# Fused attention, dense layer and routed experts: one attention chunk started a block later, expert weight splits at fixed places in the last dense group, and 13 expert steps of 256 with 2 of 128 in place of 12 with 4

## The chip, the cores and the metric

The kernel runs on one core of one Trainium2 chip. The metric is the device time of one execution in microseconds (us). TensorE (PE) does the matmuls and transposes, ScalarE (ACT) the activations and copies, VectorE (DVE) the elementwise work, GpSimd (POOL) the indirect transfers of rows, and SyncE (SP) issues the other transfers.

## What is computed

```python
f = sigmoid(f_logit)                        # q, k, v, f: 4 x 8 x 768 x 48
state = f[t] * state + outer(k[t], v[t])    # for each batch and head, t = 0..767
y[t] = q[t] @ state
x = y as rows                               # 3072 tokens of 384
h = maximum(x @ w_in, 0); x = (h * h) @ w_out          # 384 -> 2048 -> 384
logits = x @ w_gate; e = argmax(logits); gate = softmax(logits)[e]
out[token] = gate * (maximum(x @ w1[e], 0) @ w2[e])    # 8 experts, 384 -> 1024 -> 384
```

A token goes through one expert only. With the inputs of the reference the eight experts get 648, 242, 82, 602, 407, 692, 240 and 159 tokens; the kernel doesn't know this beforehand and computes its lists on the chip.

## The kernel before

**Attention** is done in 24 chunks of 128 tokens, three to a group of 384. `scores(c)` transposes the scaled keys (`pk`) and multiplies scaled queries with them (`pa`), `masked(c)` applies the causal mask on VectorE, `outputs(c)` makes the rows `y`, `state(c)` carries the state on, `decays(c)` and `scale_qk(c)` prepare the decay products of a chunk and scale its queries and keys by them. Chunks 0 to 2 are done before the main loop.

**The dense layer** follows in eight groups `g` of 384 tokens, each in 16 blocks `i` of 128 hidden columns: `moe_h` makes `ph`, `moe_act` on ScalarE `gg` (relu, square) and its parts `gh` and `gl`, `moe_out` two blocks later adds to three accumulators `po`. In group 0 the products run in plain fp32 on `w_raw`; meanwhile the weights, which come as 64-bit words, are staged (`stage_job`), made into `w_raw` on VectorE (`convert_job`, three instructions each, 16 jobs, the last 13 one in each block) and, eight blocks later, split into a rounded part `w_hi` (ScalarE copies) and the rest `w_lo` (VectorE subtracts). From group 1 on each product is the sum of three: high by high, high by low, low by high.

While the blocks of group `g` run, `attention_group(g + 1)` makes the input of the next group: a chunk starts in block `b` (`scores`, `masked`), goes on with `decays` of the next in `b + 1`, with `outputs` and `state` in `b + 2` and `scale_qk` of the next in `b + 3`. Here `b` is 0, 5 and 10 for the three chunks. `route(g)` makes the routing of the group before: small products `pl` with the gate weights, the choice of an expert, counts (`pc`) and a table of slots (`pslot`).

**The experts** run in steps of one expert each, listed in `KINDS`: a step `D` takes 256 rows and splits both weight matrices as above, a step `S` takes 128 rows and runs its first product in plain fp32 from the raw weights `rawt`, its second one split. Each has eight blocks (`step_h`: `ph`, `hh`, `hl`; `step_out`: `qo` or `qs`). A step's weights are eight parts `j` of 384 KB; `load_w` fetches a part into `rawt[j]`, `split_part` splits it into `w_hi` and `w_lo`, and only then the same buffer can be loaded for the next step. The first two steps (`NEARLY`) use counts of the groups before the last, so that their parts are loaded and split while the last dense group still runs. `lookup` and the other tables give the rows of all later steps (`pi`). Rows come and go by indirect transfers.

Of the steps in `KINDS` the last three ran only if the counts needed them (`rest`, in `extra_steps`); 12 `D` and 4 `S` always ran. A pair of halves that finds no `D` takes two `S`.

**Order.** Up to the end of the last dense group the order on PE, ACT, DVE and POOL is that of the code. In the first two steps PE's order was that of the code and the other engines' was chosen by the scheduler; from step 2 on PE and ACT keep the order of the code. In the steps the splits are placed by `split_plan`, which goes through the blocks with an assumed time for each and places a split when its load, with 4 us assumed, is due.

Of the kernel before, what the change touches and what calls it, by code (L numbers as in the profile page):

```python
# [19 lines left out]
B, H, S, D = 4, 8, 768, 48  # L20
# [12 lines left out]
ROW = DM + 1  # L33
CAP = NT
SB = 256
KINDS = "DD" + "DDDSDDSDDSDDDS" + "SSS"
NSTEP = len(KINDS)
NBLK = NE * CAP // SB
NALWAYS = NSTEP - 3
ND = KINDS.count("D") - 2  # L40
NS = KINDS.count("S")
NEARLY = 2
# [14 lines left out]
def gla_moe_moe_kernel(ctx: ExitStack, tc: tile.TileContext, qk, ft, vt, w_in, w_out, w_gate, w_gateT, w_e, q, k, v, f_logit, out, dbg=None):  # L57
# [129 lines left out]
    def convert_job(n):  # L187
        if n < len(jobs):
            w_raw[jobs[n]] = t = wlp.tile([128, WP], F32, tag="w", name="w_raw")
            narrow(t.bitcast(U32), staged.pop(n).bitcast(U32).rearrange("p (b two) -> p b two", two=2))  # L190
            stage_job(n + 3)
# [168 lines left out]
    def attention_group(g):  # L360
        for m in range(GC):
            c = g * GC + m
            b = 5 * m
            while not (yield) == (b, 1):
                pass
            if m == 0:
                x_tiles(g)
            if 4 < c + 2 < NCH:
                load_chunk(c + 2)
            scores(c)  # L370
            masked(c)
            sigmoid(c + 1)
            while not (yield) == (b + 1, 0):
                pass
            if c + 1 < NCH:
                decays(c + 1)
            while not (yield) == (b + 2, 1):
                pass
            state(c, outputs(c))
            while not (yield) == (b + 3, 0):  # L380
                pass
            if c + 1 < NCH:
                scale_qk(c + 1)
        while not (yield) == (14, 0):
            pass
        split_x(g)
        yield
# [210 lines left out]
    convert_job(1)  # L598
    decays(3)
    state(2, pu)  # L600
    convert_job(2)
    scale_qk(3)
    job = 3

    ph2 = ExitStack()
# [95 lines left out]
    def open_right():  # L701
# [42 lines left out]
        load_x(0)  # L744
        load_x(1)

    pend = []
    rt_gen = None

# [15 lines left out]

    for g in range(NG):
        att = Piece(attention_group(g + 1)) if g + 1 < NG else None
        if g == NG - 1:
            right = open_right()
        for i in range(NF):  # L770
            ph = moe_h(g, i)
            if att:
                att.at(i, 0)
            if rt_gen and 2 <= i <= 10 and g < NG - 1:
                next(rt_gen, None)
            if g == 0 and job < len(jobs):
                convert_job(job)
                job += 1
                if job == len(jobs):
                    phs.close()  # L780
                    wgp = pha.enter_context(tc.tile_pool(name="wgp", bufs=1, side="right", reuse_waits="tile"))
                    wgb = [wgp.tile([128, NE, DM], F32, name="wgb")]
                    early["ab"] = [wgp.tile([128, NBLK + SB], F32R, name=f"ab{m}") for m in range(GC)]
                    nc.sync.dma_start(out=wgb[0], in_=w_gateT[None, :, :].to_broadcast([128, NE, DM]))
            pend.append((g, i, *moe_act(g, ph)))
            n = g * NF + i - 8
            split_job(n)
            if n == len(jobs) - 1:
                wst_.extend([[w_hi[w][:, j], w_lo[w, j]] for j in range(NP)] for w in range(2))
            if len(pend) > 2:  # L790
                done = flush_one()
                if done is not None:
                    rt_gen = route(done)
                    next(rt_gen)
            if att:
                att.at(i, 1)
            if g == NG - 1:
                if i < 2:
                    next(right, None)

                for j in {5: [0], 7: [1], 9: [2], 10: [3], 11: [4], 13: [5], 15: [6, 7]}.get(i, ()):
                    split_part(*wst_[0][j], rawt[j])
                    load_w(1, j)
                if i == 13:
                    prep_step(0, *early["x0"])
            if rt_gen and i >= 2 and (i > 10 or g == NG - 1):
                next(rt_gen, None)
        if rt_gen:
            for _ in rt_gen:
                pass  # L810
            rt_gen = None
# [130 lines left out]
        nc.vector.tensor_tensor(out=need, in0=need, in1=over[:, 1:2], op=ALU.add)  # L942
        nc.vector.scalar_tensor_tensor(out=tot, in0=need, scalar=0.0, in1=bad, op0=ALU.max, op1=ALU.add)

    early["split"], early["ready"] = [], False
    SPLITS = split_plan()

    def split_w(s, j):
# [119 lines left out]
        if s < NEARLY:  # L1068
            next(fin, None)

    with tc.manual_schedule(engines={mybir.EngineType.PE}):
        left = run_steps(0, NEARLY, hook, flush=False)
    with tc.manual_schedule(engines={mybir.EngineType.PE, mybir.EngineType.Activation}):
        run_steps(NEARLY, NALWAYS, pend=left)
    more = nc.values_load(tot[0:1, 0:1], min_val=0, max_val=NSTEP + GENERAL)
    ph2.close()
    both.close()
    with tc.If(more > NS - 3, label="rest"):
        extra_steps(tc, ident, xs, x_esi, x_ids, w_e, out)
        with tc.If(more > GENERAL - 1):  # L1080
            general_path(tc, ident, rev, narrow, q, k, v, f_logit, w_in, w_out, w_gate, w_e, out)
# [4 lines left out]
def split_plan():  # L1086
# [3 lines left out]
            slots.append((clock, s, i))  # L1090
            clock += 2.0 if kind == "D" else 1.2
    begin = {(s, i): t for t, s, i in slots}
    ready, plan = {(1, j): 0.0 for j in range(8)}, {}

    def release(s, j, t):
        if s < NALWAYS:
            ready[s, j] = max(t + 4.0, begin[1, 2] if s == NEARLY else 0.0)

    for t, s, i in slots:
        if KINDS[s] == "S" and i % 2:  # L1100
            release(s + 1, i // 2, t)
# [265 lines left out]
```

## Time and profile before

| | |
|---|---|
| median of 3 runs | 817.12 us (816.12 to 817.61) |
| profiled execution | 815.93 us, of which the span on the core is 814.2 |
| TensorE busy | 782.8 us, 96% of the span |
| VectorE, ScalarE busy | 558.1 and 413.9 us |

The page lists what one profiled execution did. The busy share of an engine includes time at a reduced clock; for TensorE a window gives the granted clock as a fraction of full speed. A row of a timeline has its start, its duration, its engine and line, the tiles, and in brackets the idle time of the engine before it with what ended that.

### The profile page before, as it was taken

What the parts mean: (1) busy time and instruction counts of PE and PEld (TensorE: products, weight loads), DVE (VectorE), ACT (ScalarE), POOL (GpSimd) and SP (SyncE); (2) the same over time, 40 slices, a digit from 0 to 9 for tenths busy, and PEclk for the clock granted to TensorE, in tenths of its full rate; (3) what the DMA queues carried; (4) which work ended last, traced back from release to release, by engine and by line L of the source; (5) the groups of instructions that cost most, each with busy time, mean ns of one, the idle gap of its engine ahead of it and who ended that gap; (6) DMA issues with size and microseconds to landing.
All of it is one profiled execution on the core that took longest, in us unless ns stands there. A gap on an engine that the chain in (4) does not pass through costs nothing.

```text
span 814.2 us, 15228 instructions
## 1 busy us (share of the span) xinstructions
PE 782.8 (96%) x5681; PEld 728.7 (89%) x5681; DVE 558.1 (69%) x1315; ACT 413.9 (51%) x830; POOL 78.1 (10%) x109
## 2 busy tenths in 40 slices
PE   5699999999999999999999999999999999999995
PEld 4556569999999999999999999999999999999995
DVE  7988859767757757857757844668567565757651
ACT  2223466454454455455455454662566566556651
POOL 2000000000000000000000002000423312313111
PEclk9899999999999999999999999999999999999998
DMA  9975330121130121131120015321867686868730
GB/s 262 245 245 180 130 70 25 46 80 45 44 101 25 45 81 46 44 85 41 45 70 1 1 39 195 106 78 45 326 208 215 216 281 195 292 204 291 226 112 30
DMA packets 40564, 102.10 MB, mean 125 GB/s; under 512 B 5630, under 2 KB 9442, under 8 KB 40352
## 3 DMA queue, kind: packets, MB, share of 16 engines
q1 hardware_dynamic: 36896, 91.57, 37.2%
q0 software_dynamic: 3584, 9.46, 3.1%
q8 instruction: 47, 0.77, 0.4%
q14 instruction: 37, 0.30, 0.1%
HBM read 91.31 MB, written 10.24 MB: 125 GB/s over the span
## 4 chain that ended last, share of the span: by engine, by line
PE 75%; issue 8%; DMA 7%; DVE 4%; ACT 3%; POOL 1%; SPq 0%; POOLq 0%; DVEq 0%; ACTq 0%
PE po L434 22%; PE ph L404 21%; PE qo L997 9%; PE ph L977 8%; DMA raw<-w_e 5%; PE ph L394 4%; PE pa L263 3%; PE py L319 3%; ACT w_hi L612 2%; PE py L299 1%; PE pu L309 1%; DVE w_lo L613 1%; DMA out<-o,ids 1%; DMA xT<-xT 1%; PE pk L256 1%
## 5 line engine op out<-in xcount | busy, mean ns | idle before, releaser
L410 ACT ACTIVATE gg<-ph 128x384 f32<-128x384 f32 x128 | 62.8, 491 | 181.0 <-PE ph L404 128.1
L613 DVE TENSOR_TENSOR w_lo<-raw,w_hi 128x768 fp32r<-128x768 f32 x112 | 106.9, 956 | 47.8 <-ACT w_hi L612 44.0
L404 PE MATMUL ph<-xh,w_lo 128*128 128x384 f32 x336 | 118.6, 353 | 1.4 <-ACT gg L410 1.4
L417 DVE TENSOR_TENSOR gl<-gg,gh 128x384 fp32r<-128x384 f32 x112 | 62.0, 554 | 78.4 <-ACT gh L415 74.4
L404 PE MATMUL ph<-xl,w_hi 128*128 128x384 f32 x336 | 114.4, 340 | 0.6 <-DVE xl L162 0.6
L434 PE MATMUL po<-w_hi,gl 128*128 128x384 f32 x336 | 113.5, 338 | 1.5 <-DVE gl L417 1.5
L404 PE MATMUL ph<-xh,w_hi 128*128 128x384 f32 x336 | 113.8, 339 | 0.0
L434 PE MATMUL po<-w_hi,gh 128*128 128x384 f32 x336 | 113.2, 337 | 0.0
L434 PE MATMUL po<-w_lo,gh 128*128 128x384 f32 x336 | 112.7, 336 | 0.0
L612 ACT ACTIVATE w_hi<-raw 128x768 fp32r<-128x768 f32 x112 | 93.8, 839 | 21.2 <-DMA raw<-w_e 20.6
L981 ACT ACTIVATE hh<-ph 128x256 fp32r<-128x256 f32 (+1 forms) x128 | 45.4, 356 | 91.2 <-PE ph L977 67.4
L977 PE MATMUL ph<-xh,w_lo 128*128 128x256 f32 x288 | 82.6, 287 | 0.6 <-DVE w_lo L613 0.6
L458 DVE SCALAR_TENSOR_TENSOR junk<-rows,wgb 128x384 f32<-128x384 f32 x144 | 79.8, 554 | 3.3
L977 PE MATMUL ph<-xl,w_hi 128*128 128x256 f32 x288 | 81.2, 282 | 0.0
L977 PE MATMUL ph<-xh,w_hi 128*128 128x256 f32 x288 | 81.0, 281 | 0.0
L982 DVE SCALAR_TENSOR_TENSOR hl<-ph,hh 128x256 fp32r<-128x256 f32 (+1 forms) x128 | 49.4, 388 | 45.2 <-ACT hh L981 40.9
L404 PEld LDWEIGHTS ph<-xh,w_lo 128*128 128x128 f32 x336 | 63.0, 187 | 7.4 <-issue 3.1
L411 ACT ACTIVATE gg<-gg 128x384 f32<-128x384 f32 x128 | 67.2, 525 | 4.0
L997 PE MATMUL qo<-w_hi,hl 128*128 128x384 f32 x192 | 66.1, 344 | 1.0 <-ACT o L1009 1.0
L997 PE MATMUL qo<-w_hi,hh 128*128 128x384 f32 x192 | 65.1, 339 | 0.0
L997 PE MATMUL qo<-w_lo,hh 128*128 128x384 f32 x192 | 65.0, 338 | 0.0
L434 PEld LDWEIGHTS po<-w_hi,gl 128*128 128x128 f32 x336 | 63.0, 188 | 2.1 <-DVE gl L417 1.8
(235 smaller groups left out, 1534.4 us busy)
## 6 DMA issues: line engine op xcount, KB each, us to landing
raw<-w_e SPq DMA_DIRECT2D x128, 384.0 KB
qk<-qk SPq DMA_DIRECT2D x46, 192.0 KB
v<-vt SPq DMA_DIRECT2D x24, 256.0 KB
stg<-w_in SPq DMA_DIRECT2D x8, 768.0 KB
stg<-w_out SPq DMA_DIRECT2D x8, 768.0 KB
f<-ft SPq DMA_DIRECT2D x24, 226.2 KB
xs<-rows SPq DMA_DIRECT2D x8, 577.5 KB
wgb<-w_gateT SPq DMA_DIRECT2D x1, 1536.0 KB
```

The costliest lines, as they stand in the source:

```text
L404: nc.tensor.matmul(ph, lhsT=w[:, sl], rhs=x[:, k, :], start=(n == 0), stop=(n == 8))
L410: nc.scalar.activation(out=gg, in_=ph, func=AF.Relu)
L411: nc.scalar.activation(out=gg, in_=gg, func=AF.Square)
L417: nc.vector.tensor_tensor(out=gl, in0=gg, in1=gh.bitcast(F32), op=ALU.subtract)
L434: nc.tensor.matmul(po[m], lhsT=a[:, sl], rhs=w[:, ws], start=(i == 0 and n == 0), stop=(i == NF - 1 and n == len(terms) - 1),)
L458: nc.vector.scalar_tensor_tensor(out=junk, in0=rows[:, m, 0:DM], scalar=1.0, in1=wgb[0][:, e, :], op0=ALU.mult, op1=ALU.mult, accum_out=lg ...
L612: nc.scalar.activation(out=hi, in_=src, func=AF.Copy)
L613: eng.tensor_tensor(out=lo, in0=src, in1=hi.bitcast(F32), op=ALU.subtract)
L977: nc.tensor.matmul(ph, lhsT=wslice(s, w, (i * 3 + k) * 128, 128), rhs=x[:, k, :], start=(n == 0), stop=(n == 8))
L981: nc.scalar.activation(out=hh, in_=ph, func=AF.Relu)
L982: nc.vector.scalar_tensor_tensor(out=hl, in0=ph, scalar=0.0, in1=hh.bitcast(F32), op0=ALU.max, op1=ALU.subtract)
L997: nc.tensor.matmul(out_t[s][m], lhsT=x[:, sl], rhs=wslice(s, w, 3 * F2 + i * DM, DM), start=(i == 0 and n == 0), stop=(i == 7 and n == 2),)
```

## The change

It has three parts. First, the chunks of group 1's attention start in blocks 1, 6 and 10 of group 0 (0, 5 and 10 before), and the scaling of chunk 3 is written ahead of conversion 2. Second, the list of steps always run has 13 `D` and 2 `S`, with the two `S` at its end, and four instead of three more steps wait behind the condition. Third, a table `AHEAD` says which part of which of the first two steps is split in which block of the last dense group: (0, 3) is part 3 of step 0. Six parts of step 1 are now in it, and ACT's order in the first two steps is that of the code. `split_plan` places only parts 6 and 7 of step 1, and lets splits for step 2 begin at block 4 of step 1, not 2.

```diff
--- before.py
+++ after.py
@@ -33,10 +33,11 @@
 ROW = DM + 1
 CAP = NT
 SB = 256
-KINDS = "DD" + "DDDSDDSDDSDDDS" + "SSS"
+NEXTRA = 4
+KINDS = "DD" + "DDDDDDDDDDDSS" + "S" * NEXTRA
 NSTEP = len(KINDS)
 NBLK = NE * CAP // SB
-NALWAYS = NSTEP - 3
+NALWAYS = NSTEP - NEXTRA
 ND = KINDS.count("D") - 2
 NS = KINDS.count("S")
 NEARLY = 2
@@ -360,7 +361,7 @@
     def attention_group(g):
         for m in range(GC):
             c = g * GC + m
-            b = 5 * m
+            b = (1, 6, 10)[m] if g == 1 else 5 * m
             while not (yield) == (b, 1):
                 pass
             if m == 0:
@@ -598,8 +599,8 @@
     convert_job(1)
     decays(3)
     state(2, pu)
+    scale_qk(3)
     convert_job(2)
-    scale_qk(3)
     job = 3
 
     ph2 = ExitStack()
@@ -744,6 +745,8 @@
         load_x(0)
         load_x(1)
 
+    AHEAD = {4: [(0, 0)], 5: [(0, 1)], 6: [(0, 2)], 7: [(1, 0)], 8: [(0, 3), (1, 1)], 9: [(1, 2)], 10: [(0, 4)]}
+    AHEAD |= {11: [(1, 3)], 12: [(0, 5)], 13: [(1, 4)], 14: [(0, 6)], 15: [(0, 7), (1, 5)]}
     pend = []
     rt_gen = None
 
@@ -798,9 +801,11 @@
                 if i < 2:
                     next(right, None)
 
-                for j in {5: [0], 7: [1], 9: [2], 10: [3], 11: [4], 13: [5], 15: [6, 7]}.get(i, ()):
-                    split_part(*wst_[0][j], rawt[j])
-                    load_w(1, j)
+
+                for t, j in AHEAD.get(i, ()):
+                    split_part(*wst_[t][j], rawt[j])
+                    if t == 0:
+                        load_w(1, j)
                 if i == 13:
                     prep_step(0, *early["x0"])
             if rt_gen and i >= 2 and (i > 10 or g == NG - 1):
@@ -942,7 +947,7 @@
         nc.vector.tensor_tensor(out=need, in0=need, in1=over[:, 1:2], op=ALU.add)
         nc.vector.scalar_tensor_tensor(out=tot, in0=need, scalar=0.0, in1=bad, op0=ALU.max, op1=ALU.add)
 
-    early["split"], early["ready"] = [], False
+    early["split"], early["ready"] = [j for js in AHEAD.values() for t, j in js if t == 1], False
     SPLITS = split_plan()
 
     def split_w(s, j):
@@ -1068,14 +1073,14 @@
         if s < NEARLY:
             next(fin, None)
 
-    with tc.manual_schedule(engines={mybir.EngineType.PE}):
+    with tc.manual_schedule(engines={mybir.EngineType.PE, mybir.EngineType.Activation}):
         left = run_steps(0, NEARLY, hook, flush=False)
     with tc.manual_schedule(engines={mybir.EngineType.PE, mybir.EngineType.Activation}):
         run_steps(NEARLY, NALWAYS, pend=left)
     more = nc.values_load(tot[0:1, 0:1], min_val=0, max_val=NSTEP + GENERAL)
     ph2.close()
     both.close()
-    with tc.If(more > NS - 3, label="rest"):
+    with tc.If(more > NS - NEXTRA, label="rest"):
         extra_steps(tc, ident, xs, x_esi, x_ids, w_e, out)
         with tc.If(more > GENERAL - 1):
             general_path(tc, ident, rev, narrow, q, k, v, f_logit, w_in, w_out, w_gate, w_e, out)
@@ -1090,12 +1095,14 @@
             slots.append((clock, s, i))
             clock += 2.0 if kind == "D" else 1.2
     begin = {(s, i): t for t, s, i in slots}
-    ready, plan = {(1, j): 0.0 for j in range(8)}, {}
+    ready, plan = {(1, j): 0.0 for j in (6, 7)}, {}
 
     def release(s, j, t):
         if s < NALWAYS:
-            ready[s, j] = max(t + 4.0, begin[1, 2] if s == NEARLY else 0.0)
-
+            ready[s, j] = max(t + 4.0, begin[1, 4] if s == NEARLY else 0.0)
+
+    for j in range(6):
+        release(NEARLY, j, 0.0)
     for t, s, i in slots:
         if KINDS[s] == "S" and i % 2:
             release(s + 1, i // 2, t)
```

On VectorE, just before the main loop and in its first block, before. L166, L169 and L172 are one conversion, L234 to L236 the scaling of chunk 3, L270 its masking:

```order
43 L166 TENSOR_SCALAR w_raw<-stg 128x768
44 L169 SCALAR_TENSOR_TENSOR w_raw<-stg,w_raw 128x768
45 L172 SCALAR_TENSOR_TENSOR w_raw<-stg,w_raw 128x768
46 L234 TENSOR_TENSOR qk_148<-qk_148,tl 112x512
47 L235 TENSOR_TENSOR qk_148<-qk_148,f 112x512
48 L236 TENSOR_TENSOR pmin<-pmin,tl 112x4
49 L166 TENSOR_SCALAR w_raw<-stg 128x768
50 L169 SCALAR_TENSOR_TENSOR w_raw<-stg,w_raw 128x768
51 L172 SCALAR_TENSOR_TENSOR w_raw<-stg,w_raw 128x768
52 L270 TENSOR_TENSOR at<-pa,mask 128x512 x2
```

The same place of the changed kernel; its lines have a number one higher:

```order
43 L235 TENSOR_TENSOR qk_148<-qk_148,tl 112x512
44 L236 TENSOR_TENSOR qk_148<-qk_148,f 112x512
45 L237 TENSOR_TENSOR pmin<-pmin,tl 112x4
46 L167 TENSOR_SCALAR w_raw<-stg 128x768
47 L170 SCALAR_TENSOR_TENSOR w_raw<-stg,w_raw 128x768
48 L173 SCALAR_TENSOR_TENSOR w_raw<-stg,w_raw 128x768
49 L167 TENSOR_SCALAR w_raw<-stg 128x768
```

The scaling has moved ahead of conversion 2. The masking, ahead of which two conversions stood, follows as row 55, behind three.

On TensorE at the same place before: L394 is `ph` in group 0, L256 and L263 are the scores of chunk 3, L434 is `po`, L299 the first part of its outputs:

```order
53 L394 MATMUL ph<-xT_186,w_raw 128x384 x3
54 L256 MATMUL pk<-ident,qk_148 128x112 x4
55 L263 MATMUL pa<-qk_148 128x128 x8
56 L394 MATMUL ph<-xT_186,w_raw 128x384 x6
57 L434 MATMUL po_489<-w_raw,gg 128x384
58 L434 MATMUL po_490<-w_raw,gg 128x384
59 L434 MATMUL po_491<-w_raw,gg 128x384
60 L299 MATMUL py<-qk_148,wst_106 64x128 x8
```

After:

```order
53 L395 MATMUL ph<-xT_186,w_raw 128x384 x6
54 L257 MATMUL pk<-ident,qk_148 128x112 x4
55 L264 MATMUL pa<-qk_148 128x128 x8
56 L395 MATMUL ph<-xT_186,w_raw 128x384 x3
57 L435 MATMUL po_489<-w_raw,gg 128x384
58 L435 MATMUL po_490<-w_raw,gg 128x384
59 L435 MATMUL po_491<-w_raw,gg 128x384
60 L395 MATMUL ph<-xT_186,w_raw 128x384 x3
61 L435 MATMUL po_489<-w_raw,gg 128x384
62 L435 MATMUL po_490<-w_raw,gg 128x384
63 L435 MATMUL po_491<-w_raw,gg 128x384
64 L300 MATMUL py<-qk_148,wst_106 64x128 x8
```

Two blocks of `ph` now run ahead of the scores, and two blocks of `po` with a `ph` between them ahead of the outputs.

On ScalarE in the last blocks of group 7 and the first of step 0, before. L410, L411 and L415 are the activation of a dense block, L612 is a `w_hi` copy (154 and 155 are the buffers of the two steps' weights, the numbers of `raw` its parts), L451 takes the last accumulators, L981 is `hh` of a step and L476 the copy `xt` in the routing:

```order
538 L415 ACTIVATE gh<-gg 128x384
539 L612 ACTIVATE w_hi_155<-raw_5246 128x768
540 L410 ACTIVATE gg<-ph 128x384
541 L411 ACTIVATE gg<-gg 128x384
542 L415 ACTIVATE gh<-gg 128x384
543 L612 ACTIVATE w_hi_154<-raw_5247 128x768
544 L612 ACTIVATE w_hi_154<-raw_5248 128x768
545 L451 ACTIVATE rows<-po_5385 128x384
546 L451 ACTIVATE rows<-po_5387 128x384
547 L612 ACTIVATE w_hi_155<-raw_5247 128x768
548 L981 ACTIVATE hh<-ph_5912 128x256
549 L476 ACTIVATE xt_5258<-pt 128x384
```

After (its L613 is the same copy, L986 is `hh`):

```order
538 L416 ACTIVATE gh<-gg 128x384
539 L613 ACTIVATE w_hi_154<-raw_5247 128x768
540 L411 ACTIVATE gg<-ph 128x384
541 L412 ACTIVATE gg<-gg 128x384
542 L416 ACTIVATE gh<-gg 128x384
543 L613 ACTIVATE w_hi_154<-raw_5248 128x768
544 L613 ACTIVATE w_hi_155<-raw_5246 128x768
545 L452 ACTIVATE rows<-po_5385 128x384
546 L452 ACTIVATE rows<-po_5387 128x384
547 L986 ACTIVATE hh<-ph_5924 128x256
548 L613 ACTIVATE w_hi_155<-raw_5247 128x768
549 L477 ACTIVATE xt_5258<-pt 128x384
```

The copy of part 6 of step 0 now comes a block earlier (row 539), and a copy for step 1 no longer directly precedes the activation of the next block with its raw part just requested.

On VectorE in the first blocks of step 0, before. L513 to L518 belong to the routing of group 7, L654 and L656 to the tables of the later steps, L982 is `hl` of a step's block:

```order
713 L513 TENSOR_REDUCE sf<-sl 128x3
714 L654 TENSOR_TENSOR gt_6098<-cnt,jj_6096 128x96
715 L654 TENSOR_TENSOR gt_6104<-cnt,jj_6102 128x96
716 L515 CAST si<-sf 128x3
717 L931 TENSOR_REDUCE ctot<-cnt 128x1
718 L656 TENSOR_REDUCE nb_6100<-gt_6098 128x8
719 L656 TENSOR_REDUCE nb_6106<-gt_6104 128x8
720 L517 TENSOR_SCALAR hl<-si 128x3
721 L518 TENSOR_SCALAR hl<-si 128x3
722 L982 SCALAR_TENSOR_TENSOR hl<-ph_6034,hh 128x256
```

After:

```order
707 L514 TENSOR_REDUCE sf<-sl 128x3
708 L987 SCALAR_TENSOR_TENSOR hl<-ph_6044,hh 128x256
709 L655 TENSOR_TENSOR gt_6104<-cnt,jj_6102 128x96
710 L655 TENSOR_TENSOR gt_6110<-cnt,jj_6108 128x96
711 L516 CAST si<-sf 128x3
712 L936 TENSOR_REDUCE ctot<-cnt 128x1
713 L657 TENSOR_REDUCE nb_6106<-gt_6104 128x8
714 L657 TENSOR_REDUCE nb_6112<-gt_6110 128x8
715 L518 TENSOR_SCALAR hl<-si 128x3
716 L519 TENSOR_SCALAR hl<-si 128x3
```

`hl` of block 3 (`hl<-ph_6034` before, `hl<-ph_6044` after) has moved from behind the routing's shifts to a place ahead of `gt`.

## Rows read from the trace of the kernel before

**Rows 1.** Page, part 1: busy time of each engine, share of the span, instructions.

```profile
PE 782.8 (96%) x5681; PEld 728.7 (89%) x5681; DVE 558.1 (69%) x1315; ACT 413.9 (51%) x830; POOL 78.1 (10%) x109
```

**Rows 2.** Waits of TensorE: us in total, times, longest.

```profile
PE pk L256 <- issue: 4.8, 1, 4.8
PE po L434 <- DVE gl L417: 1.5, 1, 1.5
...
PE qo L997 <- ACT o L1009: 1.0, 1, 1.0
```

**Rows 3.** Timeline of TensorE, 28 to 62 us.

```profile
30.00 2.20 PE L394 MATMUL ph<-xT,w_raw 128*128 128x384 f32 x6 [0.64 <-ACT xT L332]
37.02 0.98 PE L256 MATMUL pk<-ident,qk 112*128 112x112 f32 x4 [4.82 <-issue]
...
39.94 5.87 PE L394 MATMUL ph<-xT,w_raw 128*128 128x384 f32 x12
...
47.67 0.67 PE L299 MATMUL py<-qk,wst 48*64 48x128 f32 x16
...
49.75 2.20 PE L394 MATMUL ph<-xT,w_raw 128*128 128x384 f32 x6
...
53.73 2.10 PE L394 MATMUL ph<-xT,w_raw 128*128 128x384 f32 x6
```

**Rows 4.** Timeline of VectorE, 32 to 40 us.

```profile
33.78 0.55 DVE L166 TENSOR_SCALAR w_raw<-stg 128x768 uint32<-128x768 uint32 x1
...
36.23 0.68 DVE L234 TENSOR_TENSOR qk<-qk,tl 112x512 f32<-112x512 f32 x1
...
37.51 0.55 DVE L166 TENSOR_SCALAR w_raw<-stg 128x768 uint32<-128x768 uint32 x1
```

**Rows 5.** Windows: length, busy by engine (PE, PEld, DVE, ACT, POOL), PEclk, DMA, GB/s.

```profile
36.60:43.50 6.90, 6.48 (x26) 4.49 (x27) 6.80 (x12) 1.07 (x2) 0.00 (x0) 0.51 0.71 233
...
106.00:110.00 4.00, 2.07 (x7) 0.94 (x6) 1.36 (x1) 2.81 (x5) 0.00 (x0) 1.00 0.12 26
```

**Rows 6.** Waits of VectorE from 32 to 96 us.

```profile
DVE at L270 <- PE pa L263: 5.0, 2, 4.7
DVE w_lo L162 <- ACT w_hi L161: 1.2, 3, 0.4
```

**Rows 7.** Timeline of TensorE: the preparations of steps 2, 4, 11 and 15.

```profile
582.69 0.82 PE L641 MATMUL px<-ident,xg 128*128 128x128 f32 x6
...
617.81 0.82 PE L641 MATMUL px<-ident,xg 128*128 128x128 f32 x6
...
726.48 0.49 PE L1034 MATMUL px<-ident,xg 128*128 128x128 f32 x3
...
789.03 0.49 PE L1034 MATMUL px<-ident,xg 128*128 128x128 f32 x3
```

**Rows 8.** Chain that ended last, 520 to 552 us: start, us, what.

```profile
545.32 3.27 DMA raw<-w_e
```

**Rows 9.** Timeline of ScalarE, 538 to 556 us.

```profile
541.23 0.85 ACT L612 ACTIVATE w_hi<-raw 128x768 fp32r<-128x768 f32 x1 [2.05 <-DMA raw<-w_e]
...
548.61 0.84 ACT L612 ACTIVATE w_hi<-raw 128x768 fp32r<-128x768 f32 x1 [2.02 <-DMA raw<-w_e]
```

**Rows 10.** Timeline of TensorE: `pl` of group 6, and of group 7.

```profile
499.67 2.07 PE L484 MATMUL pl<-wg,xt 128*128 128x8 f32 x18
...
549.03 0.73 PE L484 MATMUL pl<-wg,xt 128*128 128x8 f32 x6
...
551.99 0.52 PE L977 MATMUL ph<-xh,w_lo 128*128 128x256 f32 x1
```

**Rows 11.** Window 552 to 556 us, columns as in rows 5.

```profile
552.00:556.00 4.00, 4.00 (x27) 3.84 (x26) 2.38 (x13) 0.61 (x2) 0.00 (x0) 0.57 0.01 4
```

**Rows 12.** Timeline of VectorE, 553 to 575 us.

```profile
556.87 0.43 DVE L654 TENSOR_TENSOR gt<-cnt,jj 128x96 f32<-128x96 f32 x2
...
557.80 0.42 DVE L982 SCALAR_TENSOR_TENSOR hl<-ph,hh 128x256 fp32r<-128x256 f32 x1
```

## Prediction

> **What bounds the kernel now.** I read the busy times of the page first: TensorE is busy 782.8 us of 814.2, 96% [rows 1], so the time is the length of TensorE's own work plus its few waits and the stretches in which its clock is granted at half. The second view is therefore the list of TensorE's waits. Apart from the start, where nothing is changed, four of them lie where the change works: 4.8 us before the transposes `pk`, 1.5 us before `po`, 1.0 us before `qo` and (in the third part below) short ones before `pl` [rows 2]. The third view is the timeline around each, the fourth the windows that give the granted clock. Three places remain, and I cost them apart: attention chunk 3 in dense group 0, the list of expert steps, and the passage from the last dense group into the first expert steps.
>
> **Part 1: chunk 3 a block later, its scaling before conversion 2.** TensorE finishes block 0's `ph` near 32.2, waits 4.82 us for the transposes of chunk 3 and only then goes on [rows 3]. What is late is VectorE: it does conversion 2 (33.78 to 36.23) before it scales `kd` (from 36.23, 0.68) [rows 4]. "issue" as the releaser only says that the profile shows no nearer event; the end of the `kd` row at 36.9 fits the start at 37.02. During the wait and just after it the granted clock falls to half, 1.2 GHz: 0.51 over 36.6 to 43.5 [rows 5]. Work of 6.9 us at 0.51 would take 3.4 us less at full clock.
>
> I rebuild the stretch row by row in the new order. One block of `ph` and `po` takes 53.73 − 49.75 = 3.98 us at full clock, so a `ph` about 2.0 [rows 3]. Blocks 0 and 1 of `ph` now come first and end near 34.0. On VectorE the scaling takes the place of conversion 2: `kd` is ready at 33.78 + 0.68 = 34.5. A wait of 0.5 us is left. Scores took 39.94 − 37.02 = 2.92 us at half clock, so about 1.5 at full: until 36.0. Block 2's `ph` needs conversion 2, which now follows the three scaling rows: 33.78 + 1.28 + 2.45 = 37.51 [rows 4], a second wait of 1.5 us. Then `ph`, `po`, `ph`, `po` (7.96), the outputs of chunk 3 (49.75 − 47.67 = 2.08 [rows 3]) and `ph` of block 4 starts at 37.51 + 10.04 = 47.55, where it started at 53.73 before. **Gain 6.2 us.**
>
> The moved step takes its loads along: chunk 5's load is issued one block later on SP's queue, and its data are first read with chunk 4's scores, five blocks behind. Conversion 2 ends 1.3 us later, so does the issue of staging load 5; conversion 5 now comes after two more conversions, the masking and the scans of chunk 4, so that load keeps over 6 us. The masking of chunk 3 now stands behind conversions 3 and 4 (2.45 each): 37.51 + 4.9 = 42.4, done by 43.7; its reader, the outputs of chunk 3, is due at 45.5.  Is the gain given back later, because VectorE can't follow? From 32 to 96 us, up to the last conversion, its two largest waits are 5.0 us for `pa` and 1.2 for `w_hi` [rows 6]. So VectorE could end that conversion at most some 6.2 us earlier, which just covers the gain: after that it has no idle time left. The loads of the gate weights and of `xT` follow the last conversion and move with it.
>
> **Part 2: two steps of 128 become one of 256.** A step of 256 takes (617.81 − 582.69)/2 = 17.56 us between preparations of its rows. From 726.48 to 789.03 there are three of them and one of 128: 62.55 − 52.68 = 9.87 [rows 7]. Two of these less one of 256 is **2.18**. From 617.81 to 726.48 there are five of 256 and two of 128: 108.67 − 87.80 = 20.87, which is 1.13 over 2·9.87. A step of 128 may so cost the steps behind it something. After the change the steps of 128 are the last two, with no step of 256 behind them, so I take it that **1.13** goes too (0 at the least). Together 3.3 us. At nothing I cost: the wider step's splits and x rows (the ten such steps of before run at 17.56 with them); the weight load, one step fewer; the two adjoining steps of 128, where a load is issued per odd block and is wanted about a step later, and a load took 3.27 us [rows 8]. If that cover were gone, one load, 3.3 us, would show.
>
> Weighed against the Trainium skill ("FP8 and Floating Point Precision", TensorE Precision Notes): true fp32 goes through the array four times. Counted in columns at 2.4 GHz this gives 8·(2·(3·512 + 3·384) − (9·256 + 6·384)) = 6144 columns, an estimate of 2.56 us where the rows give 2.18; by it the gain of this part would be 3.7.
>
> **Part 3: the splits for steps 0 and 1 at fixed places.** In the last blocks of group 7 ScalarE waits 2.05 us at 541.23 in front of a `w_hi` copy whose raw weights are still on their way [rows 9]; the load behind it takes 3.27 us from release to landing [rows 8]. Everything queued behind it on ScalarE is late, first the activation of block 15, so TensorE waits 1.50 us before `po` [rows 2]. At 548.61 it happens again, 2.02 us [rows 9]; now the copy of `xt` is late, and the 18 small `pl` matmuls take 551.99 − 549.03 = 2.96 us where the group before needed 2.07 [rows 10]: 0.9. Right after, the window 552 to 556 has a granted clock of 0.57 [rows 11]; 0.86 of it at half is 3.4 us, 1.7 us lost. Later ScalarE takes a copy for step 2 ahead of `o`, and `qo` waits 0.96 [rows 2]. In the new order a block or more of other work always stands between a load and its copy, two or three in the last group, where a block takes over 3 us of TensorE time: the loads land in that time. Copies for step 2 start two blocks later, behind both `o`. So 1.5 + 0.9 + 1.7 + 1.0 = 5.1 may go.
>
> What comes in: VectorE's new order has `hl` of block 3 ahead of the two `gt` of the step tables. Before, `gt` began at 556.87 and this `hl` at 557.80 [rows 12]. VectorE must now stand until then, 0.9 us; everything on the chain to `pslot` is that much later. The bounds are 0 (TensorE reaches `pslot` early enough behind) and 0.9; the chain was tight, I take 0.75. The same lateness meets `pi`, which TensorE already waited for a little: again 0 to 0.9, I take 0.75. **Net 5.1 − 1.5 = 3.6 us,** bounds 1.5 (the clock stays low and both are paid in full) and 5.1. SP's scalar reads for the expert numbers are now ahead of step 3's loads only, and the writing of the last rows comes later; both have a step of slack.
>
> **Sum.** 6.2 + 3.3 + 3.6 = 13.1. The profiled execution took 815.93, so 802.8. The median of the three runs, 817.12, is 1.2 above it; on it the forecast is 804.0. A change under 0.2%, 1.6 us, could hardly be told from none here.
>
> **Rivals.**
>
> *The clock falls all the same.* In part 1 0.5 + 1.5 us of waiting remain within 3.6 us. For it: at 552 the clock fell after far less waiting. Against it: from 106 to 110 TensorE is busy only 2.07 of 4.00 us and keeps a clock of 1.00 [rows 5], nearly the same share. If it falls, up to 3.4 us are lost in part 1 (807.4); if it stays low in part 3, 1.7 (805.7). The Trainium skill ("TensorE: Matmul & The Clock Gate", What's actually happening) says that the slow clock is the default and activity releases it. By that rule a wait that is merely shortened can still cost the clock; 106 to 110 is a row where it did not, 552 one where it did.
>
> *VectorE or the staging loads bound group 0.* For it: VectorE's two gaps are all it can give [rows 6]. Against it: conversions run ahead of their readers, which is why `pa` let VectorE wait 5.0 us. If a staging load is late by one conversion (2.45), or the end of conversion 15 moves by half of those 6.2 only, part 1 gives 3 to 3.8, some 3.5: 806.7.
>
> *The new waits eat part 3.* If the chain to `pslot` and `pi` is late by more than the one `hl` (each further `hl` ahead of it waits for a block of TensorE, about 2 us), part 3 gives 0.5: 807.1.
>
> *The conditional rest runs: slower.* The always-run list holds 13 steps of 256 and 2 of 128. The routed counts of the reference's inputs are 648, 242, 82, 602, 407, 692, 240, 159: two pairs in early steps, 11 more and 2 single halves. Before, 10 pairs fitted and the eleventh took two steps of 128, four of four; now 11 of 11 and 2 of 2. It decides at a third half: then four extra steps of 128 run after all others. At 9.87 us each, their loads hidden, they add 39.5: 802.8 + 39.5 + 1.2 = 843.5, and more if the loads show. Both lists are filled exactly, so only an error in my count brings this.
>
> **How the numbers follow.** Forecast as summed 0.58; clock falls in part 1 or 3 0.15; VectorE or loads in group 0 0.10; new waits 0.12; rest runs or something of that size 0.03; the remaining 0.02 for no difference that can be told, for which every part would have to fail. The likeliest case alone spans 801.5 (part 3 at 5.1, part 2 at 3.7) to 806. The range 801 to 808 takes in the three rivals of the same sign with their single prices and leaves out two of them together. Faster 0.95, same 0.02, slower 0.03.
>
> **What would show it.** Part 1: `ph` of block 4 starts near 47.5, two waits of 0.5 and 1.5 stand in place of 4.82, and the clock is 1.00 from 32 to 48. Part 2: 17.56 between preparations throughout, 9.9 per step of 128 at the end. Part 3: no ScalarE wait on `raw` behind 538, `po` and `qo` out of the list of waits, `pslot` and `pi` in it with 0.7 to 1.3 each. I'm wrong if the clock is at half after chunk 3, if conversions trail their loads, or if a chain of table rows holds TensorE for over 2 us in step 0 or 1.

## The result

The changed kernel takes 804.95 us in the median of 4 runs (803.46 to 805.68), the kernel before 816.91 in the runs beside it; the ratio is 0.9864, 95% interval 0.9846 to 0.9881. Forecast were 804.0, within 801 to 808. The profiled execution took 804.5 us, with a span of 802.8 where it was 814.2: 11.4 us less, where 13.1 were forecast.

Four places of TensorE's timeline cut the span into stages: the first product of group 1, the preparations of steps 0 and 2, and the last matmul. In the changed kernel:

```profile
102.46 0.45 PE L405 MATMUL ph<-xh,w_lo 128*128 128x384 f32 x1 [0.88 <-ACT gg L411]
...
527.71 0.82 PE L642 MATMUL px<-ident,xg 128*128 128x128 f32 x6
...
572.07 0.82 PE L642 MATMUL px<-ident,xg 128*128 128x128 f32 x6
...
765.23 0.49 PE L1039 MATMUL px<-ident,xg 128*128 128x128 f32 x3
...
791.13 0.34 PE L1002 MATMUL qs<-w_hi,hh 128*128 128x384 f32 x1
```

The same rows of the kernel before that were not shown yet:

```profile
108.75 0.44 PE L404 MATMUL ph<-xh,w_lo 128*128 128x384 f32 x1 [1.36 <-ACT gg L410]
...
534.00 0.82 PE L641 MATMUL px<-ident,xg 128*128 128x128 f32 x6
...
805.05 0.34 PE L997 MATMUL qs<-w_hi,hh 128*128 128x384 f32 x1
```

| stage | before | after | less by | forecast |
|---|---|---|---|---|
| start to first product of group 1 | 108.75 | 102.46 | 6.29 | 6.2 |
| to the preparation of step 0 | 425.25 | 425.25 | 0.00 | 0 |
| to that of step 2 | 48.69 | 44.36 | 4.33 | 3.6 |
| to the end of the last matmul | 222.70 | 219.40 | 3.30 | 3.3 |
| to the end of the span | 8.81 | 11.33 | −2.52 | 0 |

TensorE was to end 13.1 us earlier and ended 13.9 earlier. Behind it 2.5 us were lost, in a stage that the prediction costed at nothing.

Timeline of TensorE at chunk 3, after; the rows answer to [rows 3]:

```profile
30.07 4.14 PE L395 MATMUL ph<-xT,w_raw 128*128 128x384 f32 x12 [0.64 <-ACT xT L333]
34.64 0.58 PE L257 MATMUL pk<-ident,qk 112*128 112x112 f32 x4 [0.43 <-PE ph L395]
35.29 1.16 PE L264 MATMUL pa<-qk 48*128 48x128 f32 x16
37.82 2.17 PE L395 MATMUL ph<-xT,w_raw 128*128 128x384 f32 x6 [1.37 <-DVE w_raw L173]
...
47.81 2.20 PE L395 MATMUL ph<-xT,w_raw 128*128 128x384 f32 x6
```

Two waits of 0.43 and 1.37 stand in place of 4.82 (forecast 0.5 and 1.5), and block 4 starts at 47.81 (forecast 47.55, before 53.73). That is 5.92 us earlier; the stage gains 6.29 mainly because the wait before the first product of group 1 also shrank, from 1.36 to 0.88. The first row covers two blocks of `ph`, which now run without a break. The window over the stretch that had a clock of 0.51 [rows 5]:

```profile
36.60:43.50 6.90, 5.68 (x18) 3.46 (x19) 6.73 (x10) 1.02 (x2) 0.00 (x0) 1.00 0.69 217
```

At the passage into the expert steps, the list of TensorE's waits has one row, and the small routing products are one group again, as long as in the group before; they answer to [rows 2] and [rows 10]:

```profile
PE pi L673 <- DVE sel L669: 1.2, 1, 1.2
```

```profile
540.94 2.07 PE L485 MATMUL pl<-wg,xt 128*128 128x8 f32 x18
```

`po` and `qo` wait no more, and the clock stays at full speed here: the window that follows the small products, which had 0.57 [rows 11], now reads

```profile
544.00:548.00 4.00, 4.00 (x37) 3.84 (x36) 3.14 (x15) 1.50 (x3) 0.00 (x0) 1.00 0.00 0
```

The list of waits doesn't show all of the 4.33 us, so they are added up from starts: from the first product of a group to the first of the next. Won are 1.77 (the last 27 `po`, 6.49 to 4.72), 1.03 (`pl`, 2.96 to 1.93), 1.54 (clock: the `ph` and `qo` behind `pl`, 3.74 to 2.20) and 1.34 (the `qo` that waited for `o`, 2.39 to 1.05), together 5.68. Paid are 0.82 (the wait for `pi`, 0.39 to 1.21) and 0.58 (`pslot`). That makes 4.28. `pslot` isn't in the list of waits, but the next `ph` starts 0.35 us behind it before (first two rows) and 0.93 after:

```profile
560.28 0.52 PE L543 MATMUL pslot<-abr 128*96 128x256 f32 x3
560.63 0.28 PE L977 MATMUL ph<-xh,w_lo 128*128 128x256 f32 x1
```

```profile
549.62 1.09 PE L544 MATMUL pslot<-abr 128*96 128x256 f32 x3
550.55 0.28 PE L982 MATMUL ph<-xh,w_lo 128*128 128x256 f32 x1
```

It is 0.92 or 0.93 in all nine traces with the third part of the change, and 0.35 or 0.36 in the four without.

### The profile page after: what moved, and what is told of

It is laid out like the page before. It is cut to its first block, busy times and chain, and to the rows that moved or that the text cites. A ratio compares the mean times of both kernels' runs of the same rounds, so it can differ in the third digit from the quotient of the medians.

```text
span 802.8 us, 15135 instructions
## 1 busy us (share of the span) xinstructions
PE 775.1 (97%) x5657; PEld 723.2 (90%) x5657; DVE 561.3 (70%) x1309; ACT 413.4 (51%) x822; POOL 76.2 (9%) x108
## 4 chain that ended last, share of the span: by engine, by line
PE 85%; issue 6%; DVE 4%; DMA 2%; POOL 1%; ACT 1%; POOLq 0%; SPq 0%; DVEq 0%; ACTq 0%
PE po L435 25%; PE ph L405 23%; PE ph L982 11%; PE qo L1002 11%; PE ph L395 3%; PE pa L264 3%; PE py L320 3%; PE py L300 1%; PE pu L310 1%; DMA xT<-xT 1%; PE px L642 1%; PE pk L257 1%; DMA out<-o,ids 1%; PE pl L485 0%; DVE tl L216 0%
## 5 line engine op out<-in xcount | busy, mean ns | idle before, releaser
L411 ACT ACTIVATE gg<-ph 128x384 f32<-128x384 f32 x128 | 62.8, 491 | 184.6 <-PE ph L405 134.0
L986 ACT ACTIVATE hh<-ph 128x256 fp32r<-128x256 f32 (+1 forms) x120 | 44.3, 370 | 103.3 <-PE ph L982 91.5
L613 ACT ACTIVATE w_hi<-raw 128x768 fp32r<-128x768 f32 x112 | 93.6, 837 | 0.0
L982 PE MATMUL ph<-xh,w_lo 128*128 128x256 f32 x312 | 88.9, 285 | 0.0
L982 PE MATMUL ph<-xl,w_hi 128*128 128x256 f32 x312 | 87.6, 281 | 0.0
L982 PE MATMUL ph<-xh,w_hi 128*128 128x256 f32 x312 | 87.5, 280 | 0.0
L1002 PE MATMUL qo<-w_hi,hl 128*128 128x384 f32 x208 | 70.4, 339 | 0.0
L1002 PE MATMUL qo<-w_hi,hh 128*128 128x384 f32 x208 | 70.4, 338 | 0.0
L1002 PE MATMUL qo<-w_lo,hh 128*128 128x384 f32 x208 | 70.1, 337 | 0.0
L405 PEld LDWEIGHTS ph<-xl,w_hi 128*128 128x128 f32 x336 | 63.1, 188 | 1.0 <-DVE xl L163 0.8
```

Of the source, the lines that this page charges most:

```text
L405: nc.tensor.matmul(ph, lhsT=w[:, sl], rhs=x[:, k, :], start=(n == 0), stop=(n == 8))
L411: nc.scalar.activation(out=gg, in_=ph, func=AF.Relu)
L613: nc.scalar.activation(out=hi, in_=src, func=AF.Copy)
L982: nc.tensor.matmul(ph, lhsT=wslice(s, w, (i * 3 + k) * 128, 128), rhs=x[:, k, :], start=(n == 0), stop=(n == 8))
L986: nc.scalar.activation(out=hh, in_=ph, func=AF.Relu)
L1002: nc.tensor.matmul(out_t[s][m], lhsT=x[:, sl], rhs=wslice(s, w, 3 * F2 + i * DM, DM), start=(i == 0 and n == 0), stop=(i == 7 and n == 2),)
```

## Experiments

### The end behind the last matmul

The instructions of the line that closes the conditional part, on GpSimd's queue, in the changed kernel (count, duration in ns, first and last start):

```profile
L1083 POOLq EVENT_SEMAPHORE  x5: 17/43/43, 793.2 to 795.9; - x5
...
L1083 POOLq COMPARE_BRANCH  x1: 45/45/45, 792.7 to 792.7; - x1
...
L1083 POOLq INC_SWDGE_SEM  x1: 1299/1299/1299, 796.0 to 796.0; - x1
```

And in the kernel before:

```profile
L1078 POOLq EVENT_SEMAPHORE  x4: 17/30/43, 807.1 to 807.3; - x4
...
L1078 POOLq COMPARE_BRANCH  x1: 45/45/45, 806.6 to 806.6; - x1
...
L1078 POOLq INC_SWDGE_SEM  x1: 1312/1312/1312, 807.4 to 807.4; - x1
```

GpSimd skips the conditional part at 792.7, meets five semaphore instructions instead of four, and the last comes at 795.9. Then it resets the semaphores of its own transfers (1.30 us) and drains (the longest of three drains takes 4.65 us). The last scatter was issued at 792.36 and took 3.5 us to land, so the fifth instruction seems to wait for this landing:

```profile
792.36 0.98 POOL L1015 DMA_INDIRECT out<-o,ids  x1 [6.56 <-ACT o L1014]
```

```profile
out<-o,ids POOLq DMA_INDIRECT x1, 3.5
```

```profile
L1370 POOLq DRAIN  x3: 40/107/4648, 797.3 to 802.5; - x3
```

The part skipped has four steps where it had three. The rival: the two steps of 128 at the end of the list make the last scatter land late. Three kernels tell them apart; the first is the changed kernel with

```diff
-NEXTRA = 4
+NEXTRA = 3
```

> The changed kernel with three extra conditional steps instead of four; nothing of them is executed. Theory E (the number of conditional steps): the end behind the last matmul falls from 11.3 to 8.8 us as in the kernel before, because GpSimd no longer waits for the last scatter ahead of its semaphore reset; the time is 2.5 us under that of the changed kernel, about 802.4. Rival S (the two steps of 128 at the end of the list make the last scatter land late): the end stays at 11.3 us and the time at 805.

It took 803.40 us (ratio 0.9847, 0.9827 to 0.9868). Last matmul and span:

```profile
790.56 0.34 PE L1002 MATMUL qs<-w_hi,hh 128*128 128x384 f32 x1
```

```profile
span 799.7 us, 15133 instructions
```

8.8 us behind the last matmul; the list of GpSimd's queue has four semaphore instructions again:

```profile
L1083 POOLq EVENT_SEMAPHORE  x4: 17/30/43, 792.6 to 792.8; - x4
...
L1083 POOLq INC_SWDGE_SEM  x1: 1296/1296/1296, 792.9 to 792.9; - x1
```

The scatter still lands 3.4 us after its issue, near 795.2, but the reset doesn't wait for it any more: it starts at 792.9, and the landing falls into the drain. By the stage theory E holds. The time of the whole kernel says less: the intervals of this run and of the changed kernel overlap.

The kernel before with four extra steps:

```diff
-KINDS = "DD" + "DDDSDDSDDSDDDS" + "SSS"
+KINDS = "DD" + "DDDSDDSDDSDDDS" + "SSSS"
-NALWAYS = NSTEP - 3
+NALWAYS = NSTEP - 4
-    with tc.If(more > NS - 3, label="rest"):
+    with tc.If(more > NS - 4, label="rest"):
```

> The kernel before with four extra conditional steps instead of three; nothing of them is executed. Theory E: all stages as before, the last matmul ends at 805.4, and the end behind it grows from 8.8 to 11.3 us: 2.5 us slower, 819.5. Rival S: no change, 817.

818.69 us, ratio 1.0033 (1.0017 to 1.0049): slower, by 2.7 us. Its profiled execution took 825.34 us, with a late start and a longer passage, so only its end is read here: from the last matmul to the end of the span 11.1 us, with five semaphore instructions:

```profile
L1078 POOLq EVENT_SEMAPHORE  x5: 17/42/43, 814.2 to 816.8; - x5
```

The list of steps is that of the kernel before, so the rival S is out.

Does the end grow with every extra step, or is it one step up? The changed kernel with `NEXTRA = 2`:

> The changed kernel with two extra conditional steps. Theory Q (the semaphores of GpSimd's transfers are used in turn, and four extra steps with their eight transfers reach that of the last scatter, three or two do not): 8.8 us behind the last matmul, as with three. Rival G (the end grows with the size of the conditional part, step by step): less than 8.8, some 6.3.

800.54 us in one run; 8.75 us behind the last matmul, with three semaphore instructions. So it is one step up between three and four. The program says why: the semaphores that the reset waits for, in the rows for GpSimd of the changed kernel (first) and of that with three extra steps, are

```
133 L1083 ISA [waits Pool_49,DMASW4_49,DMASW5_49,DMASW3_49,DMASW6_49,DMASW2_49,DMASW7_49,DMASW1_49,DMASW0_49]
130 L1083 ISA [waits Pool_49,DMASW3_49,DMASW4_49,DMASW2_49,DMASW5_49,DMASW1_49,DMASW0_49]
```

An extra step has two transfers of GpSimd, a gather and a scatter. They take eight semaphores in turn: four steps use all of them, 0 to 7, three only 0 to 5, two 0 to 3. The reset waits for those that the conditional part uses, whether it runs or not. In the programs of these kernels and of the kernel before, the last scatter ahead of the branch raises number 7 (`DMASW7_49`): the steps that always run have 28 gathers and 28 scatters in each of them, and the 56th transfer has the last of the eight. So only the fourth extra step brings the last scatter into what the reset waits for, and the landing and the end of the wait, both 795.9, agree with it.

### Part 1 alone, and its two halves

The kernel before with the two edits of part 1 and nothing else:

> The kernel before with the first part of the change alone (chunks of group 1 in blocks 1, 6, 10 and the scaling of chunk 3 ahead of conversion 2). Theory: the parts add up, so the first product of group 1 comes 6.3 us earlier, everything behind it keeps its distances, and the time is 810.6. Rival (part of the gain is given back at the passage, because the loads there come at other times): 811.5 or more.

810.98 us, ratio 0.9934 (0.9908 to 0.9961), an interval that holds both the theory's time and the rival's. From the first product of group 0 to that of group 1 72.5 us (78.75 before, 72.4 in the changed kernel), so 6.3 us are won; the passage takes 48.1 and the end 8.8, so nothing is given back there. But this execution lost 1.65 us in between: from the first product of group 1 to the preparation of step 0 it took 426.9 us, not 425.25. The clock fell there:

```profile
104.00:108.00 4.00, 4.00 (x11) 2.64 (x10) 2.23 (x4) 3.32 (x6) 0.00 (x0) 0.57 0.02 4
```

It isn't lost each time: a second trace of the changed kernel has 0.64 in this window and 426.94 us, where the first has 1.00 and 425.25. The waits around the first products of group 1 are 0.9 and 0.6 us in the first trace, 1.1 and 0.6 in the second. Here the clock fell, at 1.7 us each, in five of the nine traces with the whole of part 1 and in none of the other four; whether part 1 makes it likelier isn't shown.

Each half alone, in the kernel with three extra steps. First the scaling ahead of the conversion, with chunk 3 in block 0 again:

```diff
-            b = (1, 6, 10)[m] if g == 1 else 5 * m
+            b = 5 * m
```

> Three extra steps; of part 1 only the scaling of chunk 3 ahead of conversion 2, the chunks of group 1 again in blocks 0, 5 and 10. Theory W (the waits count, the clock holds): TensorE has one wait of 2.5 us before the scores instead of 0.4 and 1.4, so from the first product of group 0 to that of group 1 it takes 73.0 us, not 72.4. Rival C (one wait of that length drops the granted clock to half): 76.4 us and a granted clock near 0.5 from 36 to 43 us.

It gave 803.89 us in one run, and 74.65 us in this stage, between the two: more than the waits say, less than a full drop of the clock. The wait and the windows:

```profile
33.88 0.57 PE L257 MATMUL pk<-ident,qk 112*128 112x112 f32 x4 [2.37 <-issue]
```

```profile
32.00:36.00 4.00, 2.04 (x20) 1.70 (x20) 3.90 (x9) 1.63 (x4) 0.00 (x0) 0.89 0.56 186
36.00:40.00 4.00, 4.00 (x11) 2.33 (x10) 3.93 (x6) 0.49 (x1) 0.00 (x0) 0.68 0.57 176
```

The clock did fall to half, for part of the time: 4·(0.11 + 0.32) = 1.72 us lost. With the 0.6 for the longer wait, 72.3 + 0.6 + 1.7 = 74.6.

Then chunk 3 in block 1, with conversion 2 ahead of the scaling again:

```diff
-    scale_qk(3)
     convert_job(2)
+    scale_qk(3)
```

> Three extra steps; of part 1 only the chunks of group 1 in blocks 1, 6 and 10, the scaling of chunk 3 again behind conversion 2. Theory W: one wait of 2.8 us before the scores, then block 2 without a wait, 73.2 us from the first product of group 0 to that of group 1. Rival C: the clock drops, 76.6 us.

804.2 us in one run, 75.1 us in the stage. One wait of 2.88, and again 1.72 us of clock (0.68 and 0.89):

```profile
35.92 0.57 PE L257 MATMUL pk<-ident,qk 112*128 112x112 f32 x4 [2.88 <-issue]
```

```profile
36.00:40.00 4.00, 3.93 (x24) 2.61 (x25) 3.90 (x7) 1.07 (x2) 0.00 (x0) 0.68 1.00 358
40.00:44.00 4.00, 4.00 (x13) 2.36 (x12) 3.93 (x7) 1.01 (x2) 0.00 (x0) 0.89 0.91 298
```

Neither W nor C is right alone: both halves shorten the wait, and each leaves one of 2.4 or 2.9 us, behind which the clock falls for a while (one trace each). Only together do they cut it into 0.4 and 1.4 with the scores between, and there the clock stayed at 1.00 from 32 to 48 us in all nine traces that have both.

### Without part 3

The kernel with three extra steps, with the old placing of the splits of steps 0 and 1 and ScalarE left to the scheduler there:

```diff
-                for t, j in AHEAD.get(i, ()):
-                    split_part(*wst_[t][j], rawt[j])
-                    if t == 0:
-                        load_w(1, j)
+                for j in {5: [0], 7: [1], 9: [2], 10: [3], 11: [4], 13: [5], 15: [6, 7]}.get(i, ()):
+                    split_part(*wst_[0][j], rawt[j])
+                    load_w(1, j)
...
-    with tc.manual_schedule(engines={mybir.EngineType.PE, mybir.EngineType.Activation}):
+    with tc.manual_schedule(engines={mybir.EngineType.PE}):
         left = run_steps(0, NEARLY, hook, flush=False)
...
-    ready, plan = {(1, j): 0.0 for j in (6, 7)}, {}
+    ready, plan = {(1, j): 0.0 for j in range(8)}, {}
```

> The changed kernel with three extra steps and without its third part (the splits for steps 0 and 1 placed as in the kernel before, ScalarE left to the scheduler there). Theory: from the preparation of step 0 to that of step 2 it takes 48.7 us as before, not 44.4, with the clock at half for 3.4 us behind the routing's small products; 806.7. Rival (the 4.3 us come from the list of steps, which changes the splits for step 2, not from the fixed places): near 45 us and 803.

806.39 us, ratio 0.9874 (0.9848 to 0.9901). The passage takes 49.6 us, with ScalarE's waits for raw weights (2.03 and 1.98 us), the wait of 1.5 before `po` and those before `pl` all there, and the clock at half for longer than in the trace of the kernel before:

```profile
544.00:548.00 4.00, 3.46 (x19) 3.37 (x20) 3.81 (x13) 1.41 (x4) 0.00 (x0) 0.71 0.02 6
548.00:552.00 4.00, 4.00 (x25) 3.69 (x24) 1.86 (x15) 0.38 (x1) 0.00 (x0) 0.50 0.00 0
552.00:556.00 4.00, 4.00 (x28) 3.99 (x28) 3.33 (x22) 0.77 (x2) 0.00 (x0) 0.93 0.40 148
```

4·(0.29 + 0.50 + 0.07) = 3.4 us are lost, twice the 1.7 of before. In the four traces with the old placing the clock falls behind these products each time (1.7 us lost in three, 3.4 in this one), and the passage takes 48.1 to 53.1 us. In the nine with the new one it stays at 1.00 throughout the passage, which takes 44.3 to 45.0 us in the seven that have the tables in their place. So the third part wins the passage, 49.6 − 44.3 = 5.3 us here, and the list of steps doesn't. Its places and ScalarE's order were undone together; which of the two does how much isn't shown.

### One step of 128 among those of 256

```diff
-KINDS = "DD" + "DDDDDDDDDDDSS" + "S" * NEXTRA
+KINDS = "DD" + "DDDDDSDDDDDDS" + "S" * NEXTRA
```

> Three extra steps; the two steps of 128 no longer side by side, one now stands behind five steps of 256 and has six behind it. Theory L (a step of 128 delays the steps of 256 behind it): the stretch from the preparation of step 2 to the last matmul grows by 0.5 to 0.7 us over 219.35, and the step behind it takes 18.1 us between preparations in place of 17.6 less its own share. Rival N (the 1.13 us came from the splits of the old list): 219.35 as it is.

805.67 us in one run. From the preparation of step 2 to the last matmul it takes 220.8 instead of 219.35, 1.4 more; the stretch behind the lone step of 128, from its successor's preparation to the next, is 19.0 us. The list of waits holds 0.81 of it, for a `w_lo` of the step that follows; by the starts of the products this wait cost 1.07:

```profile
682.36 0.39 PE L982 MATMUL ph<-xh,w_lo 128*128 128x256 f32 x1 [0.81 <-DVE w_lo L614]
```

The direction is that of theory L, the size twice what was expected. A step of 128 reads its first product from the raw weights and hands the parts on late: ScalarE had waited 2.94 us for the raw part of this split.

```profile
680.47 0.85 ACT L613 ACTIVATE w_hi<-raw 128x768 fp32r<-128x768 f32 x1 [2.94 <-DMA raw<-w_e]
```

What the other 0.35 us are stays open.

### The wait that is left

The table of rows one block later; with it the gather for step 3 has to come one block later:

```diff
     yield
     yield
+    yield
     pi = yield from lookup(T, go, n, "1")
...
-                if i == 0 and s + 2 != NEARLY:
+                if i == (1 if s == 1 else 0) and s + 2 != NEARLY:
```

> Three extra steps; the product for the table of rows (pi) and what hangs on it one block later, and the row gather for step 3 one block later too. Theory: the wait of 1.2 us before pi goes, the splits of step 2 still find their loads landed, 43.2 us from the preparation of step 0 to that of step 2, and the time is 1.1 us under that with three extra steps. Rival: the loads of step 2, now one block later, make ScalarE's copies at block 4 of step 1 late, and 1 us or more comes back before step 2.

802.53 us, ratio 0.9828 (0.9805 to 0.9851). The wait for `pi` is gone; the passage takes 43.5 us, 0.8 less than with three extra steps, since a wait of 0.5 before `qo` is new. Its interval overlaps that of three extra steps alone. So it was run once more, beside the changed kernel on the same chip:

> The changed kernel as it is, timed on the same chip as the next one: about 1.2% under the kernel before, 11.3 us behind the last matmul.

> Three extra steps and the table of rows one block later, beside the changed kernel on the same chip. Theory: 2.5 us from the end and 0.8 us from the passage, so 3.3 us under the changed kernel. Rival (what is won at the end is lost to the spread of the start): 1.5 us or less.

The changed kernel took 805.39 us (0.9852, 0.9823 to 0.9881; the end 10.9), the other 801.46 (0.9810, 0.9781 to 0.9839; the end 8.8, the passage 42.9, this time with no wait in it). 3.9 us lie between the medians, 3.3 were expected; of the stages, the end gave 2.06 and the passage 1.45. By their medians it is the fastest kernel that was timed more than once. Its slowest run, 802.73, lies under the fastest of the changed kernel, 803.28, though the two intervals overlap.

## Why the prediction was right, and where it wasn't

*Part 1* held: the two waits, the full clock and the place of block 4 (0.26 us behind the forecast) came as rebuilt, and the stage takes 72.2 to 72.8 us in nine traces, against 78.75 before. That the gain met 6.2 to 0.1 us is luck in part, because the wait before group 1 varies from 0.7 to 1.3 us in these traces. The rival with VectorE and the staging loads is visible but small: VectorE waits 0.83 us for a staging load at 58, and nothing on TensorE follows from it. The rival with the clock didn't come at chunk 3, and the halves of part 1 show how near it was: with a wait of 2.37 us it comes. The rule of the Trainium skill ("TensorE: Matmul & The Clock Gate", What's actually happening), that activity must release the slow clock, agrees with the halves, where a shortened wait still cost 1.72 us of clock; the whole, at 1.00 throughout where [rows 5] had 0.51, shows that a wait can be cut short enough. The prediction's row against this rival, 106 to 110 at 1.00 [rows 5], was weaker than it looked: at the same place of the program the clock fell in five traces of thirteen.

*Part 2* held, 3.3 us: 17.56 us between preparations throughout, and 9.84 between the last two. The estimate by columns after the Trainium skill ("FP8 and Floating Point Precision", TensorE Precision Notes), 3.7, was too high; the rows decide. The 1.13 that steps of 128 cost those behind them were taken from sums; the lone step in the middle shows that there is such a cost, 1.4 there.

*Part 3* was mis-sized by 0.7, in the terms that go. The prediction took the waits for `po` and `qo` from the list, 1.5 and 1.0; by the starts of the products they cost 1.77 and 1.34. Together with `pl` and the clock that is 5.7 us, not 5.1. The list counts a wait from the end that the page gives the product before, and a product's row is longer than its distance to the next (0.34 us against 0.17 to 0.18 for `po`), so it shows less than was lost.

The two new waits cost 0.58 and 0.82, 1.40 where 1.5 was taken. The size held, but not the reason: the step "VectorE must now stand until then, 0.9 us" failed. VectorE stood 0.14 us before `hl`. By the rows the larger part of the lateness of `gt` came earlier, 0.76 us: a split of step 1's weights (`w_lo`) now stood ahead of `sl`, the first row that reads the counts. After:

```profile
545.07 0.18 PE L502 MATMUL pc<-oh,tri 128*128 128x8 bf16 x1
```

```profile
545.37 0.96 DVE L614 TENSOR_TENSOR w_lo<-raw,w_hi 128x768 fp32r<-128x768 f32 x1 [0.31 <-ACT w_hi L613]
546.25 0.17 DVE L510 TENSOR_TENSOR sl<-pc,base 128x24 f32<-128x24 f32 x1
...
546.75 0.18 DVE L514 TENSOR_REDUCE sf<-sl 128x3 f32<-128x24 f32 x1
547.07 0.42 DVE L987 SCALAR_TENSOR_TENSOR hl<-ph,hh 128x256 fp32r<-128x256 f32 x1
547.41 0.42 DVE L655 TENSOR_TENSOR gt<-cnt,jj 128x96 f32<-128x96 f32 x2
...
549.95 0.34 DVE L537 TENSOR_SCALAR abr<-ipos,hf 128x256 fp32r<-128x256 bf16 x1
```

Before:

```profile
555.73 0.18 PE L501 MATMUL pc<-oh,tri 128*128 128x8 bf16 x1
```

```profile
556.15 0.18 DVE L509 TENSOR_TENSOR sl<-pc,base 128x24 f32<-128x24 f32 x1 [0.75 <-PE pc L501]
...
559.74 0.34 DVE L536 TENSOR_SCALAR abr<-ipos,hf 128x256 fp32r<-128x256 bf16 x1
```

From the first `pc` to `sl` it is 0.42 us before and 1.18 after; the last `abr`, which `pslot` reads, ends 4.35 us behind `pc` before and 5.22 after. No run moves the split alone, so what it cost TensorE isn't shown apart from `hl`.

*What was missed* is the end. The prediction asked of the conditional steps only whether they run, and costed a fourth one at nothing if not. It cost 2.5 us without running. The step that failed is the rival "The conditional rest runs", which gave these steps a price only for the case that they run. That the forecast of the median came within 1 us is luck: the 0.8 us that TensorE won beyond the sum hid part of the end's 2.5, and the median lies 0.45 us above the profiled execution where the forecast had added 1.2.

## What to carry to other kernels

Look at what an engine does next when you cost a wait: here a TensorE wait of 2.4 to 4.8 us cost another 1.7 to 3.4 us by the clock, and one cut in two by useful work did not. Size a wait by the starts of the products around it, because the list of waits shows less, or nothing. A load, and the copy that needs it, want enough other work between them on the copy's engine, or everything queued there waits too. And read the end of the program as a stage of its own: a part that is skipped can still add waits to where it joins, and what stood hidden beside them is then laid in a row.

## What the runs showed that was not expected

- A conditional part with four instead of three steps made the end 2.0 to 2.6 us longer without being executed (10.9 to 11.3 us in three traces of two kernels, 8.7 to 8.9 in the other ten), since the reset of GpSimd's semaphores, 1.30 us, and its last drain, 4.65 us, then came behind the landing of the last scatter, 3.5 us after its issue, instead of beside it.
- The granted clock fell after single waits of 2.37 and 2.88 us, to 1.2 GHz, which cost 1.72 us each time. It stayed at 2.4 GHz after 0.43 and 1.37 with 1.7 us of small products between. At the passage it fell in all four traces with some 0.7 us of waits among the small routing products (and a wait of 1.5 to 1.7 before `po` ahead of them), and in none of the nine in which the same products had no waits.
- One program can go either way: at the start of group 1 the changed kernel kept the full clock in one execution and lost 1.7 us in another, with waits that differ by 0.25 us.
- The first product of group 0 starts between 28.9 and 30.2 us in twelve of the thirteen traces, whose program is the same up to there, and at 32.1 in the one of 825 us. Over a microsecond of the spread between runs can so come from the start alone.
